# Attention steps spread by weight between expert-layer items, with three blocks of work put off

## Chip, cores and metric

One core of one Trainium2 chip runs the whole program. The metric is device time in microseconds (us) for one execution; the time before is the median of ten. A span is the time from the first to the last instruction of one execution, taken by the hardware profiler. The engines are PE (TensorE: matmuls and transposes; PEld is its weight load), DVE (VectorE), ACT (ScalarE), POOL (GpSimd) and SP (SyncE, which issues transfers). Each engine runs its own instructions in order and waits for others by semaphores.

## What is computed

Sliding-window attention with a linear bias for 8 batches, 8 heads, 576 positions of width 64, then a two-matrix layer with a swish between, over all 4608 rows:

```python
# q, k, v: (8, 8, 576, 64); window 128; slopes[h] = 2 ** -(h + 1)
scores = 1 / sqrt(64) * q @ k^T
scores = where(0 <= i - j < 128, scores - slopes[h] * |i - j|, -1e9)
attn = softmax(scores) @ v                     # per batch and head
x = attn.transpose(0, 2, 1, 3).reshape(4608, 512)
h = x @ w_in                                   # (4608, 2048)
out = (h * sigmoid(beta * h)) @ w_out          # (4608, 512), float32
```

## The kernel before

**Attention.** A batch has five row blocks (four of 128 rows and one of 64). Its work is cut into steps. `TP(b, p)` (L221) transposes a pair of heads of q and k on PE, eight transposes into two PSUM tiles, each copied out by DVE (L230); `TT` (L235) does the same for the last 64 rows. `SC(b, m, p)` (L258) computes scores of a pair of heads for half of the rows (`m`) into one PSUM tile of two banks (`psum_s`, one buffer), and ACT takes the exponential. For batches 0 and 1 (below `NPE`, which is 2) a table is added by matmuls (L263) and one exponential covers the tile (L285); from batch 2 on four exponentials with a bias do it (L290) and DVE multiplies by a mask (L294). `PV(b, qb, g)` (L306) multiplies by the values of four heads (L317, L321); DVE takes the reciprocal (L326) and scales (L327). `X(b, qb)` (L333) puts a finished row block, transposed, into `XT`, a ring of 1536 columns: for batches below `NTE`, which is 3, by four PE transposes (L345) and a copy (L350, on ACT for batch 0 and on DVE for 1 and 2), and from batch 3 on by a DMA transpose that SP issues (L341).

**The layer.** Rows go in nine groups of 512. `HS(g, j)` (L355) is an H item: four matmuls of 512 columns (L362), a tanh on ACT (L367), a combine on DVE (L368). `OS(g, i, n)` (L372) is an O item: four matmuls (L378), and after every fourth item an eviction by ACT (L384) and a store (L389), queued on POOL two items later. A group has 16 H and 16 O items. H of group g needs all of the group's 512 columns in `XT`.

**Loads.** SP issues q, k and the first two batches' v as float32 (L95, L109); POOL casts them (L113, L119, L129, L141). For batch 2 and later POOL issues v itself with the cast in the transfer (`load_v`, L136). From batch 3 on q and k are transposed by DMA transposes on SP (`TD`, L246). POOL also issues the first matrix in four chunks (`load_w1`, L189) and the second in four (`load_w2`, L192), and stores results.

**Order.** PE's order is the program's order throughout. The prologue runs batch 0's attention. Then `spread(hs(0), by_pair(1), 3, 0)` (L550) places batch 1's steps evenly by their number between the 16 H items of group 0. From L557 on SP's and POOL's orders are the program's too. There batch 2's values are issued (L558, before that the planner is free to put POOL's instructions elsewhere, and these five have a place among batch 1's casts), then all 16 H items of group 1 run with nothing between (L560), then batch 2's steps between the 16 O items of group 0 and the first 8 of group 1, then batch 3's steps among group 2's H items and the rest of group 1's O items, and so on, H of one group with O of the one before. `merge` (L435) adds each batch's loads, casts and DMA transposes as further entries of the list at fixed distances ahead of its first score step; a DMA `X` comes 2.5 steps after its place. `spread` (L408) counts all entries alike.

Of the kernel before, what the change touches and what calls it, by code (L numbers as in the profile page):

```python
# [11 lines left out]
BF16 = mybir.dt.bfloat16  # L12
F32 = mybir.dt.float32
P = 128
# [3 lines left out]
def kernel(  # L18
# [10 lines left out]
    nc = tc.nc  # L29
    B, H, S, D = q.shape  # L30
# [8 lines left out]
    NTE = 3  # L39
    LA = 4  # L40
    LM = P * LA
    NQB = 5
# [3 lines left out]
    TOKG = 512  # L46
    NTG = T // TOKG
# [8 lines left out]
    NPE = 2  # L56
# [3 lines left out]
    ident = const.tile([P, P], BF16, name="ident")  # L60
# [29 lines left out]
    staged = {}  # L90
# [98 lines left out]
        nc.gpsimd.dma_start(out=W1[:, :, bass.ts(n, 512)], in_=W1v[:, :, bass.ts(n, 512)])  # L189

    def load_w2(n):
        nc.gpsimd.dma_start(out=W2[:, bass.ts(n, 4), :], in_=W2v[:, bass.ts(n, 4), :])  # L192

    def late_consts():
        for m in range(2):
# [22 lines left out]

    pts, xns = {}, {}

    def TP(b, p):  # L221
        src = staged.pop((b, p))
        for i in range(2):
            tps = psum_t.tile([P, LA, P], BF16, name="tps", tag="t")
            for a in range(LA):
                nc.tensor.transpose(
                    out=tps[:, a, :], in_=src[:, i, a, :, :].rearrange("r h d -> r (h d)"),
                    identity=ident[:],
                )
            nc.vector.tensor_copy(  # L230
                out=QK[b % 2][:, i, p, 0:LM].rearrange("c (r a) -> c r a", a=LA),
                in_=tps[:].rearrange("c a r -> c r a"),
            )

    def TT(b):  # L235
        tps = psum_t.tile([P, 2, NP, P], BF16, name="tps", tag="t")
# [96 lines left out]
    def X(b, qb):  # L333
        nq = ROWS[qb]
        xnv = xns.pop((b, qb))[:].rearrange("p h d -> p (h d)")
        tok0 = (b * S + P * qb) % XTR
        n1 = min(nq, XTR - tok0)
        parts = [(tok0, 0, n1)] + ([(0, n1, nq)] if n1 < nq else [])
        if b >= NTE:
            for at, r0, r1 in parts:  # L340
                nc.sync.dma_start_transpose(out=XT[:, :, at : at + r1 - r0], in_=xnv[r0:r1, :])  # L341
            return
        xt = psum_t.tile([P, NDM, P], BF16, name="xt", tag="t")
        for c in range(NDM):
            nc.tensor.transpose(  # L345
                out=xt[:, c, :], in_=xnv[:, c * P : (c + 1) * P], identity=ident[:]
            )
        copy = nc.vector.tensor_copy if b else nc.scalar.copy
        for at, r0, r1 in parts:
            copy(out=XT[:, :, at : at + r1 - r0], in_=xt[:, :, r0:r1])  # L350


    gts, opss = {}, {}
# [47 lines left out]
    def flush():  # L401
        for e in list(stores):
            e[0] -= 1
            if e[0] < 0:
                e[1]()
                stores.remove(e)

    def spread(moe, todo, lead=0, tail=3):  # L408
        done, n = 0, len(moe)
        for i, it in enumerate(moe):  # L410
            flush()
            it()
            to = len(todo) * (i + 1 - lead) // (n - lead - tail)
            while done < min(len(todo), to):
                todo[done]()
                done += 1

    def sc(b, m, p):
        return lambda: SC(b, m, p)

    def pv(b, qb, g):
        return lambda: PV(b, qb, g)

    def x(b, qb):
        f = lambda: X(b, qb)
        at[b, qb] = f
        if b >= NTE:
            lazy.append(f)
        return f

# [25 lines left out]

    def by_pair(b):
        return [
            lambda: TP(b, 0), lambda: TP(b, 1), sc(b, 0, 0), lambda: TT(b), sc(b, 0, 1),
            lambda: TP(b, 2), sc(b, 1, 0), lambda: TP(b, 3), sc(b, 1, 1), pv(b, 0, 0), sc(b, 0, 2),  # L460
            pv(b, 1, 0), sc(b, 1, 2), pv(b, 2, 0), sc(b, 0, 3), pv(b, 3, 0), sc(b, 1, 3),
            pv(b, 4, 0), pv(b, 0, 1), pv(b, 1, 1), x(b, 0), pv(b, 2, 1), x(b, 1), pv(b, 3, 1),
            x(b, 2), pv(b, 4, 1), x(b, 3), x(b, 4),
        ]

    def by_block(b):

        e = b - 1
        r = [pv(e, 2, 1), pv(e, 3, 1), x(e, 2), sc(b, 0, 0), x(e, 3), pv(e, 4, 1), sc(b, 0, 1),
             x(e, 4)] if e >= NTE else [sc(b, 0, 0), sc(b, 0, 1)]  # L470
        return r + [
            sc(b, 0, 2), pv(b, 0, 0), sc(b, 0, 3), pv(b, 1, 0),
            pv(b, 0, 1), sc(b, 1, 0), x(b, 0), pv(b, 1, 1), sc(b, 1, 1), x(b, 1),
            sc(b, 1, 2), pv(b, 2, 0), sc(b, 1, 3), pv(b, 3, 0), pv(b, 4, 0),
        ]

    with tc.manual_schedule(engines={mybir.EngineType.PE}):

        for sb in range(NQB):
            c = load_v(0, sb)  # L480
            if sb == 3:
                with tc.issue_after(c.ins):
                    load_w1(0)
                    load_w1(1)
        for p in range(NP):
            c = load_pair(1, p, None if p else W1[0:1, 0, 0:1])
            if p % 2:
                with tc.issue_after(c.ins):
                    load_w1(2 + p // 2)
            if p == 1:  # L490
                load_tail(1)
        for sb in range(NQB):
            c = load_v(1, sb)
            if sb == 3:
                with tc.issue_after(c.ins):
                    for n in range(4):
                        load_w2(n)
        with tc.tile_pool(name="psum_x", bufs=2, space=bass.MemoryType.PSUM) as psum_x:
            pools = [psum_x, psum_x, psum_s]

            def sc0(m, p):
                SC(0, m, p, pools[0])
                pools.append(pools.pop(0))

            w = psum_t.tile([P, 512], F32, name="w", tag="t")
            idle(w[:], 9)
            TP(0, 0)
            TP(0, 1)
            sc0(0, 0)
            load_beta()  # L510
            TT(0)
            sc0(0, 1)
            TP(0, 2)
            sc0(1, 0)
            TP(0, 3)
            sc0(1, 1)
            for m in range(2):
                sc0(m, 2)
            for m in range(2):
                sc0(m, 3)  # L520
                PV(0, m, 0)
            for qb in (2, 3, 4):
                PV(0, qb, 0)
        psum_h = ctx.enter_context(
            tc.tile_pool(name="psum_h", bufs=2, space=bass.MemoryType.PSUM))
        psum_o = ctx.enter_context(
            tc.tile_pool(name="psum_o", bufs=2, space=bass.MemoryType.PSUM))
        w = psum_s.tile([P, 2, 512], F32, name="w", tag="sps")
        for qb in range(NQB):
            c = PV(0, qb, 1, (psum_o, "ops") if qb % 2 else (psum_h, "hps"))  # L530
            idle(w[:, 0, :], 1)
            if qb:
                X(0, qb - 1)
                idle(w[:, 1, :], 1)
        X(0, NQB - 1)
        with tc.issue_after(c.ins):
            late_consts()
        for p in range(NP):
            load_pair(2, p)
            if p == 1:  # L540
                load_tail(2)

        def hs(g):
            return [lambda j=j: HS(g, j) for j in range(NFF)]

        def os(g):
            return [lambda n=n: OS(g, n // 4, n % 4) for n in range(NFF)]


        spread(hs(0), by_pair(1), 3, 0)  # L550
        steps, first = by_pair(2), {}
        for b in range(NTE, B):
            first[b] = len(steps)
            steps += by_block(b)
        steps += [pv(B - 1, 2, 1), pv(B - 1, 3, 1), x(B - 1, 2), pv(B - 1, 4, 1), x(B - 1, 3),
                  x(B - 1, 4)]
        with tc.manual_schedule(engines={mybir.EngineType.SP, mybir.EngineType.Pool}):  # L557
            for sb in range(NQB):  # L558
                load_v(2, sb)
            for it in hs(1):  # L560
                it()
            todo, o1, done = merge(steps, first), os(1), 0
            for g in range(1, NTG):
                if g == 1:
                    moe = os(0) + o1[0:8]
                    end = todo.index(at[2, NQB - 1]) + 1
                elif g == 2:
                    moe = hs(2)
                    moe = sum((moe[2 * n : 2 * n + 2] + [o1[8 + n]] for n in range(8)), [])
                else:  # L570
                    moe = sum(([a, c] for a, c in zip(hs(g), os(g - 1))), [])
                if g > 1:
                    end = len(todo)
                    if g + 1 < NTG:
                        b, r = divmod(TOKG * (g + 2) - 1, S)
                        end = todo.index(at[b, r // P]) + 1
                spread(moe, todo[done:end], 0, 3 if g == 1 else 6)
                done = end
            while stores:
                flush()  # L580
            for it in os(NTG - 1):
                it()
# [30 lines left out]
```

## Time and profile before

| | us |
|---|---|
| median of ten runs | 351.59 |
| lowest, highest | 348.35, 355.66 |
| the profiled execution | 351.01 |
| its span, first to last instruction | 349.2 |
| H items of group 0 with batch 1 | 25.28 to 61.48 |
| H items of group 1 alone | 61.48 to 75.29 |
| O of group 0 and half of group 1, with batch 2 | 75.29 to 107.94 |
| H of group 2 and the rest of O of group 1, with batch 3 | 107.94 to 140.68 |
| the last attention step on PE | 293.5 |

The page gives each engine's busy time and the span in 40 slices of 8.7 us. A stage's limit is read from that stage: the idle time of an engine, and what ended it. PE's busy digits say little of its pace, since matmuls overlap; pace is read from the starts of items: an H item alone takes 13.81 / 16 = 0.86 us.

### The profile page before, as it was taken

Reading aid. Unit: us, or ns where it says so; the run is one execution under the profiler, and the core shown is the slowest. Engines: PE = TensorE matmul, PEld = TensorE weight load, DVE = VectorE, ACT = ScalarE, POOL = GpSimd, SP = SyncE. Lnnn points to the kernel's source line nnn. Section 1 sums busy time; section 2 is a strip of 40 time slices with the busy share of each in tenths; the row PEclk is TensorE's granted clock in tenths of the full one; section 3 lists DMA queues with packets and bytes.
Section 4 is the critical chain, followed back from the end, with each engine's and each line's share of the span. In section 5 each row is a group of like instructions: output and inputs, shape, how many; then the busy total and the mean of one; then the engine's idle time right before and its main releaser. Section 6 shows DMA issues by size and latency. Waiting matters only on the chain.

```text
span 349.2 us, 6129 instructions
## 1 busy us (share of the span) xinstructions
PE 324.5 (93%) x2237; PEld 154.1 (44%) x2279; DVE 197.3 (57%) x421; ACT 211.3 (61%) x407; POOL 107.6 (31%) x173
## 2 busy tenths in 40 slices
PE   6988967989997989999999999999999999999995
PEld 2454424444453344444444444444444444444442
DVE  6476728686653676565566656765666464444400
ACT  4655843657725695678568756876588654544411
POOL 7638545113364431323316332432000000100000
PEclk9899989999999899999999999999999999999999
DMA  7999999961999998999639994994123002010021
GB/s 198 238 172 248 172 236 220 221 146 46 171 187 215 205 167 163 168 164 158 138 82 202 173 211 111 171 180 93 40 68 61 31 32 68 30 62 30 30 88 65
DMA packets 138494, 47.67 MB, mean 137 GB/s; under 512 B 125648, under 2 KB 135904, under 8 KB 138464
## 3 DMA queue, kind: packets, MB, share of 16 engines
q1 hardware_dynamic: 103520, 31.15, 49.0%
q0 software_dynamic: 34912, 16.13, 35.0%
q8 instruction: 18, 0.29, 0.4%
q14 instruction: 12, 0.10, 0.1%
q10 hardware_dynamic: 32, 0.01, 0.0%
HBM read 36.71 MB, written 9.44 MB: 132 GB/s over the span
## 4 chain that ended last, share of the span: by engine, by line
PE 53%; DMA 19%; issue 10%; POOL 7%; SPq 4%; DVE 3%; ACT 3%; POOLq 0%
PE ops L378 24%; PE hps L362 23%; DMA fst<-in_q_dram 8%; DMA fst<-in_v_dram 5%; DMA fst<-in_k_dram 3%; POOL bst L129 3%; PE sps L277 3%; SPq L249 2%; ACT pt L290 2%; POOL vs L136 2%; DMA W<-in_moe_w_in_dram 2%; PE pv L321 1%; SPq L109 1%; PE pv L317 1%; DVE gT L368 1%
## 5 line engine op out<-in xcount | busy, mean ns | idle before, releaser
L367 ACT ACTIVATE sig<-hps,beta_h 128x512 bf16<-128x512 f32 x144 | 99.5, 692 | 80.5 <-PE hps L362 75.7
L362 PE MATMUL hps<-XT,W 128*128 128x512 bf16 x559 | 144.4, 383 | 1.3 <-DVE gT L368 0.3
L378 PE MATMUL ops<-W,gT 128*128 128x512 bf16 x555 | 142.4, 380 | 1.3 <-issue 0.3
L368 DVE SCALAR_TENSOR_TENSOR gT<-sig,hps 128x512 bf16<-128x512 bf16 x144 | 98.4, 684 | 69.1 <-ACT sig L367 68.8
L290 ACT ACTIVATE pt<-sps,bias 128x256 bf16<-128x256 f32 (+1 forms) x192 | 75.2, 479 | 11.9 <-PE sps L277 11.8
L362 PEld LDWEIGHTS <-W 128*128 128x128 bf16 x576 | 52.5, 98 | 59.1 <-issue 4.8
L378 PEld LDWEIGHTS <-gT 128*128 128x128 bf16 x576 | 52.2, 98 | 57.8 <-issue 2.4
L389 POOL DMA_DIRECT2D out_dram<-osb x32 | 17.9, 559 | 170.4 <-ACT osb L384 170.3
L294 DVE TENSOR_TENSOR pt<-pt,mask 128x1024 bf16<-128x1024 bf16 x48 | 35.8, 745 | 24.2 <-ACT pt L290 24.2
L129 POOL CAST bst<-fst 128x512 bf16<-128x512 f32 (+1 forms) x50 | 31.9, 659 | 26.6 <-DMA fst<-in_q_dram 20.2
L384 ACT ACTIVATE osb<-ops 128x512 f32<-128x512 f32 x36 | 21.7, 603 | 26.3 <-PE ops L378 26.3
L327 DVE TENSOR_TENSOR xn<-pv,zs 128x256 bf16<-128x256 f32 (+1 forms) x80 | 33.5, 420 | 2.1
L321 PE MATMUL pv<-vs,pt 128*128 128x65 bf16 x320 | 29.3, 195 | 4.2 <-POOL vs L141 2.1
L326 DVE RECIPROCAL zs<-pv 128x4 f32<-128x4 f32 (+1 forms) x80 | 14.0, 176 | 28.7 <-PE pv L321 28.0
L277 PE MATMUL sps<-qkT 64*128 64x256 bf16 (+2 forms) x320 | 26.0, 258 | 4.4 <-ACT pt L290 3.8
L321 PEld LDWEIGHTS <-pt 128*128 128x128 bf16 x320 | 21.9, 98 | 11.9 <-DVE pt L294 2.5
L317 PE MATMUL pv<-vs,pt 128*128 128x65 bf16 x256 | 24.5, 194 | 1.4 <-DVE xn L327 1.0
L136 POOL DMA_DIRECT2D vs<-in_v_dram x30 | 25.5, 854 | 0.5 <-issue 0.4
L277 PEld LDWEIGHTS <-qkT 64*128 64x128 bf16 x320 | 11.3, 95 | 31.5 <-issue 30.1
L317 PEld LDWEIGHTS <-pt 128*128 128x128 bf16 x256 | 19.8, 98 | 11.2 <-issue 3.1
L285 ACT ACTIVATE pt<-sps 128x1024 bf16<-128x1024 f32 x16 | 16.0, 1027 | 11.5 <-PE sps L277 11.1
L113 POOL CAST bst<-fst 128x512 bf16<-128x512 f32 x24 | 14.6, 623 | 11.7 <-DMA fst<-in_q_dram 6.5
(45 smaller groups left out, 103.7 us busy)
## 6 DMA issues: line engine op xcount, KB each, us to landing
fst<-in_q_dram SPq DMA_DIRECT2D x32, 256.0 KB, 4.5
fst<-in_k_dram SPq DMA_DIRECT2D x32, 256.0 KB, 5.1
out_dram<-osb POOLq DMA_DIRECT2D x32, 256.0 KB, 3.0
vs<-in_v_dram POOLq DMA_DIRECT2D x24, 128.0 KB, 5.9
fst<-in_v_dram SPq DMA_DIRECT2D x8, 256.0 KB, 7.7
W<-in_moe_w_in_dram POOLq DMA_DIRECT2D x4, 512.0 KB, 7.9
W<-in_moe_w_out_dram POOLq DMA_DIRECT2D x4, 512.0 KB, 15.2
fst<-in_q_dram SPq DMA_DIRECT2D x8, 128.0 KB, 5.2
```

What stands on the lines that cost most here:

```text
L129: nc.gpsimd.tensor_copy(out=t[0 : ROWS[sb], i], in_=f)
L136: nc.gpsimd.dma_start(out=VS[b % 2][0 : ROWS[sb], sb, :, 0:D], in_=v[b, :, P * sb : P * sb + ROWS[sb], :].rearrange("h p d -> p h d"),)
L277: nc.tensor.matmul(o, lhsT=qk[64 * e : 64 * e + 64, 1, p, P * kb : P * kb + P], rhs=qk[64 * e : 64 * e + 64, 0, p, P * kb : P * kb + nq], ...
L290: nc.scalar.activation(out=pt[:, e, cols], in_=sps[:, e, cols], func=ACTF.Exp, scale=qscale, bias=bias[:, half, h : h + 1],)
L294: nc.vector.tensor_tensor(out=pt[:], in0=pt[:], in1=masks[m][:].rearrange("p (o c) -> p o c", o=1).broadcast_to([P, 2, 512]), op=ALU.mult,)
L317: nc.tensor.matmul(pv[:, hl, 0 : D + 1], lhsT=weights(b, qb - 1, h, 1), rhs=vs[:, qb - 1, h, 0 : D + 1], start=True, stop=False,)
L321: nc.tensor.matmul(pv[:, hl, 0 : D + 1], lhsT=weights(b, qb, h, 0), rhs=vs[:, qb, h, 0 : D + 1], start=qb == 0, stop=True,)
L327: nc.vector.tensor_tensor(out=xn[0:nq, 4 * g : 4 * g + 4, :], in0=pv[0:nq, :, 0:D], in1=zs[0:nq].broadcast_to([nq, 4, D]), op=ALU.mult,)
L362: nc.tensor.matmul(hps[:], lhsT=W1[:, c, bass.ts(j, P)], rhs=XT[:, c, c0 : c0 + TOKG], start=(c == 0), stop=(c == NDM - 1),)
L367: nc.scalar.activation(out=sig[:], in_=hps[:], func=ACTF.Tanh, scale=beta_h[:, j : j + 1])
L368: nc.vector.scalar_tensor_tensor(out=gts[g][:, j, :], in0=sig[:], scalar=1.0, in1=hps[:], op0=ALU.add, op1=ALU.mult)
L378: nc.tensor.matmul(ops_[:], lhsT=gT[:, j, i * P : i * P + P], rhs=W2[:, j, :], start=(j == 0), stop=(j == NFF - 1),)
```

## The change

Transposing a pair is cut in two steps, one for q and one for k. Every step has a weight: 2 for a score step, 1 for a transpose step, a PV step or an X done on PE, 0 for loads and DMA transposes. `spread` places steps so that the weight done keeps pace with the items done, leaves `lead` items at the start and `tail` at the end without steps, and puts anything left after the last item. Batch 1's last row block (two PV and one X) is put off to group 1's H items. Group 1's H items are no longer alone: they form one list with group 0's O items and the first 8 of group 1, and batch 2's steps run among all 40. Batch 2's steps up to X of row block 2 are due there; the PV steps and X of its last row block and one PV and X of the fourth go in front of batch 3's. X goes by DMA transpose from batch 2 on, and the PE form copies on ACT. Batch 2's values are issued behind the second matrix. The last `tail` grows from 6 to 7 for later groups.

```diff
     def load_w2(n):
-        nc.gpsimd.dma_start(out=W2[:, bass.ts(n, 4), :], in_=W2v[:, bass.ts(n, 4), :])
+        return nc.gpsimd.dma_start(out=W2[:, bass.ts(n, 4), :], in_=W2v[:, bass.ts(n, 4), :])
...
-    def TP(b, p):
-        src = staged.pop((b, p))
-        for i in range(2):
-            tps = psum_t.tile([P, LA, P], BF16, name="tps", tag="t")
...
+    def TP(b, p, i):
+        src = staged[b, p]
+        tps = psum_t.tile([P, LA, P], BF16, name="tps", tag="t")
...
-        if b >= NTE:
+        if b >= NPE:
             for at, r0, r1 in parts:
                 nc.sync.dma_start_transpose(out=XT[:, :, at : at + r1 - r0], in_=xnv[r0:r1, :])
             return
...
-        copy = nc.vector.tensor_copy if b else nc.scalar.copy
         for at, r0, r1 in parts:
-            copy(out=XT[:, :, at : at + r1 - r0], in_=xt[:, :, r0:r1])
+            nc.scalar.copy(out=XT[:, :, at : at + r1 - r0], in_=xt[:, :, r0:r1])
...
+    cost = {}
+
     def spread(moe, todo, lead=0, tail=3):
-        done, n = 0, len(moe)
+        total, n = sum(cost.get(f, 0) for f in todo), len(moe) - lead - tail
+        done, k = 0, 0
         for i, it in enumerate(moe):
             flush()
             it()
-            to = len(todo) * (i + 1 - lead) // (n - lead - tail)
-            while done < min(len(todo), to):
-                todo[done]()
-                done += 1
+            while k < len(todo) and (i + 1 - lead >= n or (
+                done + cost.get(todo[k], 0)) * n <= total * (i + 1 - lead)):
+                done += cost.get(todo[k], 0)
+                todo[k]()
+                k += 1
+        for f in todo[k:]:
+            f()
+
+    def step(f, c):
+        cost[f] = c
+        return f
+
+    def tp(b, p, i):
+        return step(lambda: TP(b, p, i), 1)
+
+    def tt(b):
+        return step(lambda: TT(b), 1)
 
     def sc(b, m, p):
-        return lambda: SC(b, m, p)
+        return step(lambda: SC(b, m, p), 2)
 
     def pv(b, qb, g):
-        return lambda: PV(b, qb, g)
+        return step(lambda: PV(b, qb, g), 1)
 
     def x(b, qb):
-        f = lambda: X(b, qb)
+        f = step(lambda: X(b, qb), int(b < NPE))
         at[b, qb] = f
-        if b >= NTE:
+        if b >= NPE:
             lazy.append(f)
         return f
...
     def by_pair(b):
         return [
-            lambda: TP(b, 0), lambda: TP(b, 1), sc(b, 0, 0), lambda: TT(b), sc(b, 0, 1),
-            lambda: TP(b, 2), sc(b, 1, 0), lambda: TP(b, 3), sc(b, 1, 1), pv(b, 0, 0), sc(b, 0, 2),
-            pv(b, 1, 0), sc(b, 1, 2), pv(b, 2, 0), sc(b, 0, 3), pv(b, 3, 0), sc(b, 1, 3),
-            pv(b, 4, 0), pv(b, 0, 1), pv(b, 1, 1), x(b, 0), pv(b, 2, 1), x(b, 1), pv(b, 3, 1),
-            x(b, 2), pv(b, 4, 1), x(b, 3), x(b, 4),
+            tp(b, 0, 0), tp(b, 0, 1), sc(b, 0, 0), tp(b, 1, 0), tp(b, 1, 1), tt(b), sc(b, 0, 1),
+            tp(b, 2, 0), sc(b, 1, 0), tp(b, 2, 1), sc(b, 1, 1), tp(b, 3, 0), pv(b, 0, 0),
+            tp(b, 3, 1), sc(b, 0, 2), pv(b, 1, 0), sc(b, 1, 2), pv(b, 2, 0), sc(b, 0, 3),
+            pv(b, 3, 0), sc(b, 1, 3), pv(b, 0, 1), pv(b, 1, 1), x(b, 0), pv(b, 2, 1), x(b, 1),
+            pv(b, 3, 1), x(b, 2), x(b, 3), pv(b, 4, 0), pv(b, 4, 1), x(b, 4),
         ]
 
     def by_block(b):
 
         e = b - 1
-        r = [pv(e, 2, 1), pv(e, 3, 1), x(e, 2), sc(b, 0, 0), x(e, 3), pv(e, 4, 1), sc(b, 0, 1),
-             x(e, 4)] if e >= NTE else [sc(b, 0, 0), sc(b, 0, 1)]
+        if e < NTE:
+            r = [sc(b, 0, 0), pv(e, 3, 1), x(e, 3), pv(e, 4, 0), sc(b, 0, 1), pv(e, 4, 1), x(e, 4)]
+        else:
+            r = [pv(e, 2, 1), pv(e, 3, 1), x(e, 2), sc(b, 0, 0), x(e, 3), pv(e, 4, 1),
+                 sc(b, 0, 1), x(e, 4)]
...
-        spread(hs(0), by_pair(1), 3, 0)
-        steps, first = by_pair(2), {}
+        s1, s2 = by_pair(1), by_pair(2)
+        spread(hs(0), s1[:-3], 3, 2)
+
+        steps, first = s1[-3:] + [f for f in s2[:-3] if f not in (s2[-6], s2[-4])], {}
...
-            for sb in range(NQB):
+            with tc.issue_after(w2.ins):
+                load_v(2, 0)
+            for sb in range(1, NQB):
                 load_v(2, sb)
-            for it in hs(1):
-                it()
...
                 if g == 1:
-                    moe = os(0) + o1[0:8]
-                    end = todo.index(at[2, NQB - 1]) + 1
+                    moe = hs(1) + os(0) + o1[0:8]
...
-                if g > 1:
-                    end = len(todo)
-                    if g + 1 < NTG:
-                        b, r = divmod(TOKG * (g + 2) - 1, S)
-                        end = todo.index(at[b, r // P]) + 1
-                spread(moe, todo[done:end], 0, 3 if g == 1 else 6)
+                end = len(todo)
+                if g + 1 < NTG:
+                    b, r = divmod(TOKG * (g + 2) - 1, S)
+                    end = todo.index(at[b, r // P]) + 1
+                spread(moe, todo[done:end], 6 if g == 1 else 0, 7)
                 done = end
```

More of the change, by code (lines that the diff above doesn't have):

```diff
@@ L219 @@
     pts, xns = {}, {}
-    def TP(b, p):
-        src = staged.pop((b, p))
-        for i in range(2):
-            tps = psum_t.tile([P, LA, P], BF16, name="tps", tag="t")
[L225 to L232, printed above, removed]
-            )
+    def TP(b, p, i):
+        src = staged[b, p]
+        tps = psum_t.tile([P, LA, P], BF16, name="tps", tag="t")
+        for a in range(LA):
+            nc.tensor.transpose(
+                out=tps[:, a, :], in_=src[:, i, a, :, :].rearrange("r h d -> r (h d)"),
+                identity=ident[:],
+            )
+        nc.vector.tensor_copy(
+            out=QK[b % 2][:, i, p, 0:LM].rearrange("c (r a) -> c r a", a=LA),
+            in_=tps[:].rearrange("c a r -> c r a"),
+        )
     def TT(b):
@@ L496 @@
                     for n in range(4):
-                        load_w2(n)
+                        w2 = load_w2(n)
         with tc.tile_pool(name="psum_x", bufs=2, space=bass.MemoryType.PSUM) as psum_x:
@@ L506 @@
             idle(w[:], 9)
-            TP(0, 0)
-            TP(0, 1)
+            TP(0, 0, 0)
+            TP(0, 0, 1)
+            TP(0, 1, 0)
+            TP(0, 1, 1)
             sc0(0, 0)
@@ L512 @@
             sc0(0, 1)
-            TP(0, 2)
+            TP(0, 2, 0)
+            TP(0, 2, 1)
             sc0(1, 0)
-            TP(0, 3)
+            TP(0, 3, 0)
+            TP(0, 3, 1)
             sc0(1, 1)
```

## The prediction

> **What bounds the kernel now.** I read the page's busy shares first, then the busy times by stage, then the longest waits of TensorE (PE) stage by stage, then the order of PE and GpSimd (POOL) around each of those waits.
>
> The page's first two parts (engine, busy us, share, instructions; then tenths of 40 slices):
>
> ```profile
> PE 324.5 (93%) x2237; PEld 154.1 (44%) x2279; DVE 197.3 (57%) x421; ACT 211.3 (61%) x407; POOL 107.6 (31%) x173
> PE   6988967989997989999999999999999999999995
> PEclk9899989999999899999999999999999999999999
> ```
>
> PE is the bound, but its holes lie in the first 16 slices (up to 140 us); after that it is full and its clock is whole. The same by stage. I cut at the first hidden product H(0) (25.28), the first of H(1) (61.48), the first output product O(0) (75.29), the first of H(2) (107.94) and the first of H(3) (140.68):
>
> ```profile
> 25.28:61.48 36.20, 29.28 (x249) 14.92 (x253) 22.91 (x62) 19.50 (x25) 21.40 (x33) 0.95 1.32 223
> 61.48:75.29 13.81, 13.76 (x66) 6.26 (x64) 9.91 (x15) 10.29 (x15) 2.46 (x4) 1.00 0.98 188
> 75.29:107.94 32.65, 30.20 (x264) 16.12 (x268) 19.98 (x44) 15.92 (x39) 13.47 (x21) 1.00 1.21 150
> 107.94:140.68 32.74, 28.70 (x202) 12.87 (x205) 20.72 (x42) 24.91 (x54) 11.70 (x16) 0.95 1.20 178
> ```
>
> Columns: stretch, length, busy PE, PEld, DVE, ACT, POOL, granted PE clock, DMA share, GB/s. I call the stages A, B, C, D, and what follows E. A loses 6.9 us of PE time to idling and 5% of its clock; B loses nothing; C loses 2.4; D loses 4.0 and again 5%. In A DMA runs over its full share (1.32). In D ACT is busy 24.91 of 32.74 us, so it is nearly the second bound there. Two waits with what follows them, on PE:
>
> ```profile
> 46.76 0.19 PE L317 MATMUL pv<-vs,pt 128*128 128x65 bf16 x1
> 49.07 0.19 PE L321 MATMUL pv<-vs,pt 128*128 128x65 bf16 x1 [2.12 <-POOL vs L141]
> 50.56 1.89 PE L362 MATMUL hps<-XT,W 128*128 128x512 bf16 x4
> ...
> 111.21 0.39 PE L277 MATMUL sps<-qkT 64*128 64x256 bf16 x4
> 113.26 0.39 PE L277 MATMUL sps<-qkT 64*128 64x256 bf16 x4 [1.66 <-ACT pt L290]
> 114.76 1.90 PE L362 MATMUL hps<-XT,W 128*128 128x512 bf16 x4
> ```
>
> The first waits for a row block of batch 1's values; the second is a score step put straight behind another, with one PSUM buffer that four exponentials must empty. After each, four matmuls take 1.9 us where they take 1.03 elsewhere. The clock in those places:
>
> ```profile
> 50.00:51.00 1.00, 0.98 (x8) 0.45 (x9) 0.72 (x2) 0.33 (x1) 1.00 (x2) 0.50 1.10 351
> 115.00:116.00 1.00, 1.00 (x3) 0.30 (x2) 0.97 (x3) 0.84 (x2) 0.41 (x1) 0.50 2.05 179
> ```
>
> So a wait of about 2 us is paid twice: 5% of 36.2 is 1.8 us in A, 5% of 32.74 is 1.6 in D. Why the values were late, on POOL:
>
> ```profile
> 38.67 0.70 POOL L136 DMA_DIRECT2D vs<-in_v_dram  x1
> 43.17 0.61 POOL L141 CAST vs<-fst 128x512 bf16<-128x512 f32 x1 [1.88 <-DMA fst<-in_v_dram]
> 48.41 0.62 POOL L141 CAST vs<-fst 128x512 bf16<-128x512 f32 x1 [4.62 <-DMA fst<-in_v_dram]
> ```
>
> Batch 1's values arrive 2.5 us apart and the fourth 5.2, while batch 2's (L136, issued at 27.08, 31.34, 32.77, 34.75, 38.67) share the DMA engines.
>
> **The change part by part.** Prices of steps on PE, from start to start in its timeline: an H or O item 0.864 (13.81 / 16), four transposes 0.23, a score step 0.33 (batch 1, with table matmuls: 0.85), a PV step 0.24.
>
> Batch 2's values behind W2. This takes five POOL issues of 0.84 (4.2 us) and their transfers out of 27 to 50 us and puts them between the last casts of batch 2's q and k. On POOL's DMA queue W1's third chunk landed at 38.67, three V loads at 41.13, 43.30, 45.15, W1's last chunk at 48.89; without them the last needs 48.89 - 45.15 = 3.7 us after 38.67, about 42.4. Batch 1's fourth value block at the former 2.5 us spacing is there at 45.6, perhaps before. PE, faster by the other parts, wants the last W1 chunk at about 46 and that block at about 44. So of 2.12 + 0.36 idle and 1.8 of clock I give back 1.0 idle and 0.9 clock. What is late next: W2 (landed 59.26 to 70.41) and, behind it, batch 2's values.
>
> Transposes of q and k split in halves, each behind other work. In A it removes the waits of 0.79 (POOL's cast) and 0.81 (DVE's copy) at 30 and 31 us: 1.6. In C it removes 0.79 + 0.22. A second H item now always lies between score steps of batch 1, which removes 0.77 at 45.0. The copies themselves (0.68 each on DVE) stay; in A DVE is busy 22.91 of 36.20, which covers them. If A shrinks to 30 us, that is three quarters.
>
> Batch 1's X copies go from DVE (four of 0.41 and one of 0.29) to ACT (0.59 and 0.37): ACT gains 2.7 us in A and B, where it has 19.50 of 36.20 and 10.29 of 13.81; on the path only the copy just before H(1): two H items (1.73) cover it, and I take 0. X(1,3) still follows closely on its PV, so the wait of 1.02 at 61.15 stays; 0.41 + 0.24 go.
>
> Batch 1's last blocks (two PV, one X with its four transposes) move from A to B: 2 x 0.24 + 0.23 = 0.7 less in A, 0.7 more in B.
>
> Batch 2's X as DMA transposes. Off PE: five times 0.23 = 1.15 in C. Off DVE: 1.9. Added to SP: five issues of 1.21 (6.1 us), landing 3.3 us after issue at the median, 6.7 at most. X(2,1) and X(2,2) stand behind the two transposes of batch 3's last rows, which wait for a POOL cast, which stands behind the third store, which waits for ACT. The third store can go about 12 items (10.5 us) before H(2); then value issue and cast 2.0, two transposes 2.4, two X 2.4, landing 2 to 4: done 0 to 2 us ahead of H(2). I take 0, bounds 0 and +3.
>
> H(1) joined with O(0) and half of O(1): 40 items hold what 24 held, less two PV (0.5) moved to D, plus the first score step of batch 3 (0.33). C waited 1.2 us in four places for ACT between score steps with one O item between (a score step's four exponentials are 4 x 0.478 = 1.9); now two O items or one with transposes lie between most. Of C's 2.2 us of waits I take 1.4 as gone. B + C: -1.15 - 1.4 + 0.7 + 0.33 - 0.5 = -2.0; bounds -3 and +1.
>
> D. The two adjacent score steps are gone: -1.66 and the clock, -1.6. One score step less, two PV more: +0.2. But the new order still has seven score steps with one to three items between, and ACT needs 1.9 + 0.69 for each H item, 2.6 to 3.3 us, against PE's 1.5 to 3.2: the remaining 2.1 us of waits stay, and I add 0.6. D: -2.5; bounds -5.2 (all waits and the clock) and +2 (waits of about 1 us at most score steps).
>
> E. Waits there are only 2.1 us. By the instruction order five pairs of score steps have just one H and one O item between, three before: two times about 0.3 us. E: +0.5; bounds -1.5 and +2.
>
> A: -1.6 - 0.77 - 1.5 (values) - 0.9 (clock) - 0.65 - 0.7 = -6.1; bounds -8 (all but the 1.02) and -1.5 (loads hold PE).
>
> Sum: -6.1 - 2.0 - 2.5 + 0.5 = -10.1. The profiled execution took 351.01 (span 349.2, 1.8 around it): 340.9. It lies 0.6 under the median 351.59, so I predict **341.5**.
>
> Two pages of the Trainium skill speak otherwise. "TensorE: Matmul & The Clock Gate", section "HAM oscillation — how this bites in real kernels", says that idle gaps up to some 3.4 us leave the clock alone. The rows above show 0.50 after gaps of 2.12 and 1.66; by the page none of the 2.5 us of clock would come back, and the sum would be 344. "VectorE: DVE Perf Modes", section "Rules for kernel authors", says to transpose 128x128 on TensorE if PSUM will do, and by DMA otherwise, which is against moving batch 2's X. Here four cost PE 0.23 us and a DMA transpose lands 3.3 after its issue; by the page the 1.15 would not be worth the wait, and the sum would be about 342.7.
>
> **Rivals.** *Loads hold stage A.* PE gets ahead of W1 and batch 1's values; A gives only -1.5: 346. For it: the DMA share of 1.32 in A and 12.2 us from issue to landing of W1's last chunk. Against it: the three V loads that leave are just those ahead of that chunk.
>
> *Batch 2's values too late.* If W2's last chunk lands at 70.4 as before and five V loads follow at 2.1 us each, the last lands at 81; the first PV of batch 2 comes about 22 us after H(1) begins, near 77. About 3 us of waiting and 1.5 of clock: 346. Against it: batch 1's values, and so W2's issue behind them, come earlier.
>
> *X of batch 2 holds H(2): slower.* If the cast of batch 3's last rows is caught behind stores (POOL has stood 12.09 us at one, until 84.17), X(2,2) follows a store three further on, each about 3.5 to 4 us: 12 us later, plus clock 1.6. 341.5 + 13.5 = 355. It decides once X(2,2) lands more than 10 us after H(2) could begin; up to there it only eats the gain.
>
> *Weights change the order and not the waits:* B to D give nothing, and A what its loads allow (-1.5): about 350.
>
> **How the numbers follow.** Forecast 0.58, its own range 335.5 to 344.5 (the bounds of A and D do not fall together). Loads 0.17, values 0.10, nothing gained 0.07, X late 0.08. Range **335.5 to 348.5**, which reaches over the two middle rivals. A measurement can tell 0.5% (349.8 and 353.3) from no change: faster 0.84, same 0.08, slower 0.08.
>
> **What would show it.** A some 30 us long, no wait on values at its two thirds, PE clock whole there; W1's last chunk landed before 46 us; no DVE copy into XT; in D no wait over 1.2 us for exponentials and a whole clock; H(2) starting without a wait for a DMA. I am wrong if PE waits on W, vs or XT at those places, if D stays above 32 us, or if E grows by over 2 us.

## The result and the profile after

The changed kernel takes 348.55 us (median of 15 runs, 343.83 to 350.27), the kernel before 351.84 (median of 52, 347.82 to 355.66). The ratio is 0.9875, with an interval of 0.9842 to 0.9908: faster by 1.25%, where 341.5 us would have been 2.9%. Medians here are of all executions and ratios of those in the faster of two states alone, so a ratio is not the quotient of two medians. The median lies 0.05 us above the range: on which side of that edge it fell is chance, with single executions from 343.83 to 350.27, but the 7 us to the forecast are not. The profiled execution took 348.75 us, with a span of 346.3 and a mean granted clock of 0.979.

The page of the changed kernel first: the span, the engines' busy shares, PE's busy tenths and granted clock by slices of 8.7 us, and the group of H matmuls with the idle time ahead of it.

```profile
span 346.3 us, 6108 instructions
...
PE 323.0 (93%) x2216; PEld 152.9 (44%) x2259; DVE 194.0 (56%) x411; ACT 213.6 (62%) x412; POOL 106.6 (31%) x173
...
PE   5989998999998894999999999999999999999995
PEclk9699999999999997899999999999999999999999
...
L360 PE MATMUL hps<-XT,W 128*128 128x512 bf16 x556 | 144.4, 383 | 5.5 <-DMA XT<-xn 4.6
```

The holes of the first ten slices are mostly gone. A new one has come: the 16th slice (130 to 139 us) is only four tenths busy, it and the next have a lowered clock, and the group's line names a wait of 4.6 us for a DMA into XT, which the kernel before did not have.

The stages, cut at the same instructions as before: H(0) at 26.67, H(1) at 55.46, O(0) at 73.24, H(2) at 99.67, H(3) at 134.50 us. E is in two lines, so that its clock can be seen. Columns: stretch, length, busy time of PE, PEld, DVE, ACT and POOL, granted clock, DMA share, GB/s.

```profile
26.67:55.46 28.79, 26.29 (x229) 13.63 (x233) 19.71 (x52) 20.79 (x28) 17.09 (x28) 1.00 1.19 239
55.46:73.24 17.78, 17.07 (x120) 8.60 (x121) 15.58 (x27) 13.32 (x25) 7.16 (x10) 1.00 1.51 174
73.24:99.67 26.43, 25.98 (x199) 12.44 (x201) 12.76 (x30) 15.00 (x37) 12.67 (x19) 1.00 1.47 198
99.67:134.50 34.83, 27.19 (x213) 12.73 (x216) 22.14 (x46) 24.08 (x51) 15.19 (x22) 0.99 1.20 182
134.50:142.07 7.57, 7.57 (x29) 2.93 (x30) 1.97 (x4) 1.37 (x2) 0.00 (x0) 0.61 1.42 157
142.07:346.30 204.23, 197.07 (x1232) 91.21 (x1256) 106.19 (x205) 125.03 (x246) 39.41 (x63) 1.00 0.60 98
```

Set against the stages of before and the forecast of each (us):

| stage | before | after | change | forecast |
|---|---|---|---|---|
| up to H(0) | 25.28 | 26.67 | +1.39 | 0 |
| A | 36.20 | 28.79 | -7.4 | -6.1 |
| B + C | 46.46 | 44.21 | -2.25 | -2.0 |
| D | 32.74 | 34.83 | +2.1 | -2.5 |
| E | 208.5 | 211.8 | +3.3 | +0.5 |
| around the span | 1.8 | 2.45 | +0.65 | 0 |

The table's changes sum to -2.3, which is 351.01 to 348.75. A, B and C did what was forecast, and a little more. Up to H(0) the kernels do the same work; that point lay between 26.0 and 27.9 us in the other profiles of this study, so the +1.39 is not put down to the change. The difference is in D and E. PE's timeline there (start, duration, line, and in brackets the idle time before and what ended it):

```profile
128.89 1.03 PE L376 MATMUL ops<-W,gT 128*128 128x512 bf16 x4
134.50 1.86 PE L360 MATMUL hps<-XT,W 128*128 128x512 bf16 x4 [4.58 <-DMA XT<-xn]
136.16 1.91 PE L376 MATMUL ops<-W,gT 128*128 128x512 bf16 x4
```

D ends with 4.58 us of waiting, and four matmuls then take 1.86 us, not 1.03. Without the wait D is 30.25 us, 2.5 less than before: the forecast. With a clock of 0.61 over 7.57 us, E pays 0.39 x 7.57 = 2.95 us; the remaining +0.35 stands against a forecast of +0.5. The miss in this pair of profiles is thus one wait and what follows it, 4.58 + 2.95 = 7.5 us.

What the wait hung on is shown by the chain of waits of the changed kernel, between 121 and 135 us (start, duration, what):

```profile
122.09 0.97 SPq L340
...
123.11 3.76 DMA fst<-in_q_dram
...
126.99 0.61 POOL bst L129
...
127.81 0.62 POOL bst L129
128.44 1.64 SPq L248
...
130.18 1.22 SPq L248
...
131.50 2.87 DMA XT<-xn
...
134.50 1.86 PE hps L360 x4
```

Read backwards: H(3) needs X(3,2), the third row block of batch 3 put into XT (a join, for short), a DMA transpose on SP. SP issued it at 131.50, straight behind the two transposes (L248) of a later batch's row block. Those waited for POOL's casts, and these for a load that SP had issued at 123.11, behind other transposes and an X. So SP's stream, in which loads, TD and X stand in one fixed order, had come to this step too late. In the kernel before, the same step stood at the same place of that stream:

```profile
133.24 2.83 SPq L249 DMA_TRANSPOSE qkT<-bst  x2
136.17 3.41 SPq L341 DMA_TRANSPOSE XT<-xn  x2
```

There it landed at 139.37, and H(3) began at 140.68: a margin of 1.3 us, while PE was forecast to reach H(3) some 10 us sooner.

### The profile page after: what moved, and what is told of

It reads as the page before. It is cut to its first block, busy times and chain, and to the rows that moved or that the text cites. A ratio compares the mean times of both kernels' runs of the same rounds, so it can differ in the third digit from the quotient of the medians.

```text
span 346.3 us, 6108 instructions
## 1 busy us (share of the span) xinstructions
PE 323.0 (93%) x2216; PEld 152.9 (44%) x2259; DVE 194.0 (56%) x411; ACT 213.6 (62%) x412; POOL 106.6 (31%) x173
## 4 chain that ended last, share of the span: by engine, by line
PE 82%; DVE 5%; DMA 4%; ACT 4%; issue 2%; SPq 2%; another core or an unknown queue 1%; POOL 1%; POOLq 0%
PE hps L360 33%; PE ops L376 33%; PE sps L276 6%; PE pv L320 3%; PE sps L262 2%; PE pv L316 2%; ACT pt L289 2%; DVE xn L326 2%; PE tps L225 2%; DMA fst<-in_k_dram 2%; DVE pt L293 2%; ACT sig L365 1%; DMA fst<-in_q_dram 1%; DVE gT L366 1%
## 5 line engine op out<-in xcount | busy, mean ns | idle before, releaser
L293 DVE TENSOR_TENSOR pt<-pt,mask 128x1024 bf16<-128x1024 bf16 x48 | 34.3, 714 | 14.6 <-ACT pt L289 14.3
L129 POOL CAST bst<-fst 128x512 bf16<-128x512 f32 (+1 forms) x50 | 30.9, 637 | 35.5 <-DMA fst<-in_q_dram 18.9
L229 DVE COPY qkT<-tps 128x512 bf16<-128x512 bf16 x24 | 16.2, 687 | 6.6 <-PE tps L225 6.4
```

Of the source, the lines that this page charges most:

```text
L129: nc.gpsimd.tensor_copy(out=t[0 : ROWS[sb], i], in_=f)
L293: nc.vector.tensor_tensor(out=pt[:], in0=pt[:], in1=masks[m][:].rearrange("p (o c) -> p o c", o=1).broadcast_to([P, 2, 512]), op=ALU.mult,)
```

## The experiments

All runs are compared with runs of the kernel before on the same chip, whose medians were 353.0, 352.8 and 352.3 us in the three sets.

| run | what | us | ratio to before (interval) |
|---|---|---|---|
| changed kernel | | 348.55 | 0.9875 (0.9842 to 0.9908) |
| e1_x_before_td | X(3,2) ahead of the two transposes | 347.37 | 0.9889 (0.9807 to 0.9971) |
| e2_x2_on_pe | batch 2's X back on PE | 343.78 | 0.9794 (0.9730 to 0.9858) |
| e3_v2_early | batch 2's values as before | 350.25 | 0.9966 (0.9920 to 1.0012) |
| e4_warm | PE kept busy during the wait | 348.78 | 0.9911 (0.9844 to 0.9977) |
| x2_twice | batch 2's X issued twice | 356.14 | 1.0135 (1.0074 to 1.0196) |
| x2_three_dma | three of batch 2's X by DMA | 343.78 | 0.9777 (0.9734 to 0.9821) |
| tail_11 | steps of H(2) end sooner | 346.36 | 0.9827 (0.9794 to 0.9860) |
| before_v2_late | before, values behind W2 | 348.33 | 0.9888 (0.9862 to 0.9915) |
| e2_equal_weights | e2, every entry weighs 1, loads too | 344.99 | 0.9825 (0.9773 to 0.9876) |
| e2_pairs_unsplit | e2, q and k transposed together | 345.25 | 0.9834 (0.9786 to 0.9882) |
| e2_v2_early | e2, batch 2's values as before | 348.14 | 0.9867 (0.9825 to 0.9910) |
| e2_x_sooner | e2, lag of the DMA joins 1.5 | 344.14 | 0.9765 (0.9733 to 0.9796) |

**Is it the place of X(3,2) on SP's queue, or the amount of work there?** The theory was that the five added issues hold back the whole stream; the rival, that X(3,2) has merely an unlucky place. (The expectation counts the rival as theory 1.)

```
 # e1_x_before_td, in merge
-                jobs.append((i + 2.5, f))
+                jobs.append((i + 2.4, f))
```

> The changed kernel with one number altered: a DMA transpose X comes 2.4 instead of 2.5 steps after its place, which only turns ties, so that X(3,2) stands on SP ahead of the two transposes of batch 5's first rows (TD(5,0)) and not behind them. Theory 1 (X(3,2) was late because of its place on SP): it issues some 3 us earlier (128.4 instead of 131.5), PE's wait of 4.58 us at the first H item of group 3 falls to 1 to 2 us and most of the halved clock after it (0.61 over 7.6 us, 3 us) goes: span 340 to 343. Theory 2 (X(3,2) is late because its input or SP's whole stream is late): the wait stays above 3 us, span 345 to 347.

Two lines of PE's timeline in this run:

```profile
131.01 1.02 PE L360 MATMUL hps<-XT,W 128*128 128x512 bf16 x4 [1.17 <-DMA XT<-xn]
...
200.99 1.03 PE L360 MATMUL hps<-XT,W 128*128 128x512 bf16 x4 [3.23 <-DMA XT<-xn]
```

X(3,2) was issued at 127.02, and the wait before H(3) fell to 1.17 us. But H(5) now waits 3.23 for its X, with half the clock behind it, and a third wait of 1.16 follows at 237. The span is 346.3 us, as in the changed kernel and not the 340 to 343 of theory 1, and the ratio can't be told from the changed kernel's. The place decides which group waits; the delay of the stream remains.

```
 # e2_x2_on_pe, in X and in x
-        if b >= NPE:
+        if b >= NTE:
...
-        f = step(lambda: X(b, qb), int(b < NPE))
+        f = step(lambda: X(b, qb), int(b < NTE))
```

> The changed kernel with batch 2's X back on PE (20 transposes, copies on ACT), so SP has five transposes fewer, 6 us of issuing. Theory A (those five held up SP's stream, and X(3,2) with it): SP comes to X(3,2) 3 to 6 us earlier, the wait before H(3) falls under 1.5 us, the clock stays whole there, PE pays 1.15 us for the transposes: span 340 to 342. Theory B (SP waits for loads and casts anyway, so its length does not matter): X(3,2) is issued within 1.5 us of 131.5, the wait stays above 3 us, and the span is 347 to 348.

SP's timeline in this run, then stage D and the stretch around H(3) (columns as above):

```profile
125.25 2.86 SPq L248 DMA_TRANSPOSE qkT<-bst  x2
128.21 3.33 SPq L340 DMA_TRANSPOSE XT<-xn  x2
```

```profile
99.02:132.09 33.07, 28.65 (x233) 13.61 (x237) 22.26 (x48) 25.55 (x56) 11.82 (x17) 1.00 1.12 166
132.00:140.00 8.00, 7.76 (x48) 3.43 (x47) 4.22 (x8) 5.23 (x12) 3.47 (x5) 1.00 1.19 176
```

With the five joins on PE and ACT, X(3,2) is issued 3.3 us sooner, H(3) begins at 132.09 without a wait, and the clock stays whole. The span falls by 4.8 us to 341.5 and not by the 7.5 of the wait and the clock, since the joins cost PE something too: B to D takes 43.90 + 33.07 = 76.97 us here, and 44.21 + 30.25 = 74.46 in the changed kernel without its wait. The ratio falls from 0.9875 to 0.9794, and the intervals just overlap (0.9842 to 0.9858). The next two runs vary the amount.

```
 # x2_twice, in X, after the DMA transpose
+    scr = const.tile([P, NDM, P], BF16, name="scr")
...
+                if b == 2:
+                    nc.sync.dma_start_transpose(out=scr[:, :, 0 : r1 - r0], in_=xnv[r0:r1, :])
 # x2_three_dma, in place of b >= NPE in X and in x
+    def by_dma(b, qb):
+        return b >= NTE or b == 2 and qb < 3
```

> The changed kernel with each DMA transpose X of batch 2 issued a second time, into a scratch tile that nothing reads: SP gets five more transposes (6 us of issuing, and a wait of up to 3 us where two follow each other). If SP's own stream sets when X(3,2) is issued, it comes 5 to 9 us later than 131.5, PE's wait before H(3) grows from 4.6 to 9 to 13 us, and the span is 350 to 356. If loads and casts set it, X(3,2) comes within 2 us of 131.5 and the span stays within 2 us of 346.3.

> The changed kernel with batch 2's last two X back on PE and the first three still DMA transposes: SP has three more than with none, two fewer than the changed kernel (2.4 us). If each costs SP its issue, X(3,2) comes 2 to 3 us earlier than 131.5 and PE's wait before H(3) is 1 to 2.5 us, between 4.6 (all five) and 0 (none): span 342 to 345. If it takes none of them or all to matter, the wait is 0 or still above 4.

PE's timeline of the doubled kernel (the extra copies go to a tile that nobody reads), and X(3,2) on its SP:

```profile
101.59 1.04 PE L363 MATMUL hps<-XT,W 128*128 128x512 bf16 x3 [2.14 <-DMA XT<-xn]
...
141.26 1.01 PE L363 MATMUL hps<-XT,W 128*128 128x512 bf16 x2 [8.03 <-DMA XT<-xn]
```

```profile
138.54 2.52 SPq L341 DMA_TRANSPOSE XT<-xn  x2
```

And of the kernel with three:

```profile
132.13 1.02 PE L363 MATMUL hps<-XT,W 128*128 128x512 bf16 x4 [0.44 <-DMA XT<-xn]
```

Zero, three, five and ten DMA transposes of batch 2 give a wait before H(3) of none, 0.44, 4.58 and 8.03 us, and with ten also 2.14 before H(2), the place that the prediction had looked at. Doubling makes the kernel slower than before, 1.35% over it. The doubled run changes SP's queue alone, and X(3,2) is issued 7.0 us later, for 6 us of added issuing (part may come by way of PE, which the wait before H(2) holds up). That such issues push X(3,2) back, and that H(3) then waits for it, is shown.

The waits are not the dose itself, for PE does not come to H(3) at the same time in the four kernels. Counted from each one's H(0), with none, three, five and ten:

| us after H(0) | none | three | five | ten |
|---|---|---|---|---|
| X(3,2) landed | 105.1 | 104.3 | 107.7 | 114.7 |
| PE was ready for H(3) | 105.8 | 104.0 | 103.2 | 107.0 |

Three cost X(3,2) nothing that can be seen (so the wait was 0.44 and not the expected 1 to 2.5), five 2.6 us and ten 9.7. The other half of the 4.58 us is that PE, freed of the joins, is ready 2.5 us sooner than with none. With ten it is late itself, after its wait before H(2), which is why the wait is under the expected 9 to 13.

**Does the half clock cost what the profile shows?** PE was given 21 matmuls on zeros ahead of H(3), into a buffer that nobody reads.

```
 # e4_warm, in the loop over groups
+                if g == 3:
+                    w = psum_t.tile([P, 512], F32, name="w", tag="t")
+                    idle(w[:], 21)
```

> The changed kernel with 21 matmuls on zeros, 512 columns each (4.5 us), before the first H item of group 3; they add nothing to the result. PE then has no idle time there, and the wait itself stays. If the halved clock from 134 to 141 us comes from that wait's idling, the clock stays 1.00 there and the span falls by about 3 us, to 343 to 344. If the clock falls for another reason, the span stays 346 to 348 and the clock in the stretch is again near 0.6.

PE's timeline and the stretch behind it:

```profile
129.72 4.70 PE L214 MATMUL w<-zero 128*128 128x512 bf16 x21
```

```profile
134.50:142.00 7.50, 7.37 (x46) 3.22 (x46) 3.37 (x7) 4.36 (x9) 0.00 (x0) 1.00 1.36 194
```

In the profile H(3) begins at 134.25 (134.50 in the changed kernel), the clock stays whole, and the span falls by 3.2 us to 343.1, as expected. The 12 timed runs do not show it (344.89 to 353.67, median 348.78). Five of the 12 have a mean clock of 0.981 to 0.985 all the same. The runs of the changed kernel themselves speak for the price: of the sixteen executions on record, nine with a mean clock of 0.978 to 0.983 have a median span of 347.1, seven with 0.990 to 0.995 of 344.2. That is a correlation and not an intervention, and what the zero matmuls cost in the other executions wasn't seen. So the 2.95 us is what one profile shows; over all runs it stays open.

**Would ending H(2)'s steps sooner do?**

```
 # tail_11
-                spread(moe, todo[done:end], 6 if g == 1 else 0, 7)
+                spread(moe, todo[done:end], 6 if g == 1 else 0, 11 if g == 2 else 7)
```

> The changed kernel with group 2's steps done four items (3.5 us) earlier, 11 items without steps at the end instead of 7; SP's order is the same. If X(3,2) is late because it waits for its own PV steps, it comes some 3 us earlier and the wait falls to 1 to 2 us (span 342 to 344, less 0 to 2 us of new waits for exponentials in stage D). If SP's stream ahead of it sets the moment, X(3,2) stays at 131 to 132 and the span at 345.5 to 348.

PE's waits between 95 and 142 us in this run (engine, line and releaser; total, times, longest):

```profile
PE sps L276 <- ACT pt L289: 2.1, 3, 0.7
PE hps L360 <- DMA XT<-xn: 1.2, 1, 1.2
```

X(3,2) did not come sooner (131.93). Denser score steps made PE wait for ACT instead (2.1 us, where the changed kernel has 0.9 in D), so it arrived later, waited 1.24 us and kept its clock. X(3,2) thus kept the moment that the second theory gives, while the profile's span of 343.3 is the first theory's; PE's own lateness hides the wait, which was not foreseen.

**What are the other parts worth?** Batch 2's values were put back to their old place in the changed kernel and in e2, and moved alone in the kernel before.

```
 # e3_v2_early and e2_v2_early
-            with tc.issue_after(w2.ins):
-                load_v(2, 0)
-            for sb in range(1, NQB):
+            for sb in range(NQB):
                 load_v(2, sb)
 # before_v2_late: the same lines the other way, in the kernel before
```

> The changed kernel with batch 2's five value transfers back among batch 1's casts. My account of stage A says that their moving took away the wait for batch 1's fourth value block, 2.5 us, and the clock of 1.8: stage A (26.7 to 55.5) would be 3 to 5 us longer again. If the end is set by X(3,2) on SP, less of it shows in the whole: span 346 to 349. If instead stage A was shortened by the split transposes and the weights alone, stage A stays within 1 us of 28.8 and the span within 1 us of 346.3.

> The version with batch 2's X on PE, with batch 2's values back among batch 1's casts. There is no wait for X before H(3) to hide it, so what the move is worth shows in the whole: the wait of 2.7 us for batch 1's values comes back, with or without a halved clock after it (1.8): span 344 to 346.5, median ratio 0.5 to 1.3% above that version's 0.979. If it stays under 342.5 the move is worth nothing.

> The kernel before with one part alone of the change: batch 2's values behind W2. Stage A loses the wait for batch 1's values (2.5 us) and the halved clock after it (1.8): span 349.2 - 3 to 4.5 = 344.5 to 346.5, if all else follows. In the kernel before X(3,2) landed 1.3 us before the first H item of group 3; if SP's stream sets that moment and does not move up with PE, a wait of 1 to 3 us for XT appears there and the span is 346.5 to 348.5.

PE's timeline of e3, and stage A of before with only the values moved:

```profile
49.62 0.19 PE L320 MATMUL pv<-vs,pt 128*128 128x65 bf16 x1 [2.66 <-POOL vs L141]
```

```profile
26.03:58.31 32.28, 27.80 (x248) 14.41 (x252) 22.91 (x63) 19.43 (x25) 19.79 (x32) 1.00 1.19 248
```

With the old place the wait for batch 1's values is back, 2.66 us and longer than the 2.12 before, because PE, counted from H(0), comes 0.9 us sooner and the values only 0.3. Stage A is 31.73 us long, 2.9 more than in the changed kernel; this time the clock stayed whole behind the wait. Moved alone, the values shorten A from 36.2 to 32.3 us and give the kernel a ratio of 0.9888, nearly the whole measured gain of the full change. What lies behind stage A takes 287.7 us in the kernel before and 287.8 in this run. There H(3) waits too, 1.07 us for X(3,2), with no join of batch 2 on SP: PE was ready for it at 136.24 and not at 140.68, 4.4 us sooner, and X(3,2) landed only 2.2 us sooner, at 137.22. In e2 the move is worth 0.9867 - 0.9794 = 0.7%, with overlapping intervals.

```
 # e2_equal_weights, in spread
-        total, n = sum(cost.get(f, 0) for f in todo), len(moe) - lead - tail
+        total, n = len(todo), len(moe) - lead - tail
...
-                done += cost.get(todo[k], 0)
+                done += 1
 # e2_pairs_unsplit, in by_pair (tp2 does both halves in one step of weight 2)
+            tp2(b, 0), tp2(b, 1), sc(b, 0, 0), tt(b), sc(b, 0, 1), tp2(b, 2), sc(b, 1, 0),
...
 # e2_x_sooner, in merge
-                jobs.append((i + 2.5, f))
+                jobs.append((i + 1.5, f))
```

> The version with batch 2's X on PE, with every entry of the list counted alike (loads and DMA transposes too), as the kernel before did; the order of steps and all else stay. If the weights carry part of the gain: adjacent or nearly adjacent score steps come back, PE's waits for exponentials grow by 2 to 4 us in stages B to D, perhaps with a halved clock: span 343.5 to 347 against 341.5. If the weights do not matter, the span stays within 1 us of 341.5.

> The version with batch 2's X on PE, with the transposes of a pair of heads again one step (q and k together, weight 2) in the former order. My step took 1.6 us in stage A and 1.0 in C for the split. With it undone: waits of PE for DVE's copies and POOL's casts of 0.7 to 2.6 us come back, span 342 to 344. If the join with H(1) and the weights had already spread them, the span stays within 0.7 us of 341.5.

> The version with batch 2's X on PE, with each DMA transpose X one step sooner (1.5 instead of 2.5 after its place), so most stand ahead of the neighbouring transposes of q and k. That version has no wait for XT left, so I expect nothing: span 341 to 342. If X in front makes SP wait for its input and holds loads back, new waits come later: span 342.5 to 345.

Equal weights are 0.3% and unsplit pairs 0.4% above e2, both within the intervals: neither part has a price that these runs can tell from none, though the profile of the unsplit kernel has waits of 0.81, 0.88 and 0.67 us at 32.5, 42.2 and 68.8 back. A smaller lag changes nothing. The versions e2, x2_three_dma and e2_x_sooner (0.979, 0.978, 0.977) can't be told apart; they are the fastest here, about 2% under the kernel before, and the last two lie below the changed kernel with no overlap.

## Why the prediction was wrong

**The step that failed** is "Batch 2's X as DMA transposes", with its "I take 0, bounds 0 and +3". The five issues were priced by whether X(2,1) and X(2,2) would be in time for H(2). They were: X(2,2) landed at 98.89 and H(2) began at 99.67, inside the forecast "0 to 2 us ahead". But the issues also push back what stands behind them on SP: loads, the transposes of the next batches, and X(3,2) for H(3). The prediction asked this for H(2) alone. The margin could be read from the trace of before: X(3,2) landed at 139.37, H(3) at 140.68. A PE forecast to come 10.6 us sooner there (6.1 + 2.0 + 2.5) had 1.3 us of cover, unless SP's stream came sooner too. It did, but by less: X(3,2) landed 5.0 us sooner, at 134.36, and 8.0 sooner in e2, at 131.40. So the term taken as 0 was 4.58 us of waiting and, in the profile, 2.95 of clock, of which taking the joins back to PE returned 4.8. Part of it would probably have come without them, as the 1.07 us of before_v2_late show: the gain itself uses up the margin. e2 takes 343.78 us, near the upper end of the forecast's own range.

**What held.** Stage A: -7.4 for -6.1. W1's last chunk landed at 42.35 (forecast 42.4), the fourth block of batch 1's values was cast at 43.99 (forecast 45.6 or before), and PE did not wait for it. The clock there is whole. The move of the values was under-sized: alone the move shortens A by 3.9 us, where 1.5 + 0.9 was forecast for it, and the other edits take the remaining 3.5, where 3.7 was forecast. Taken out of the changed kernel (e3) it is worth 2.9; there the clock behind the wait stayed whole. B + C: -2.25 for -2.0. D without the one wait: -2.5 as forecast (in e2, which has no wait for XT, D takes 33.07 us, two of the joins on PE included), and PE's idle time there besides that wait is 34.83 - 27.19 - 4.58 = 3.06 us, where 4.0 - 1.66 + 0.6 = 2.9 was forecast. It has changed its kind: score steps wait 0.9 for ACT (2.6 before), PV steps 1.6 for their masks (0.6 before). E without the clock: +0.35 for +0.5.

**The rivals.** "Loads hold stage A" fell: no wait for W or values in A. "Batch 2's values too late" fell: the last landed at 75.03, and the first PV of batch 2 began at 78.87. "Weights change the order and not the waits" fell with A to C, though the runs of e2 show no separate price for weights or splitting. "X of batch 2 holds H(2)" had the right mechanism, a join caught behind other work on SP and the clock after it, but one group too early: in the changed kernel it costs 7.5 us in the profile and eats the gain, and only with ten issues did it make the kernel slower.

**The two pages.** The Trainium skill, "VectorE: DVE Perf Modes", section "Rules for kernel authors", prefers TensorE for a 128x128 transpose if PSUM will do. The prediction priced that rule at 1.2 us and set it aside; here it was right for the five together, e2 against the changed kernel, though for a reason that the rule does not give: the queue, not the transpose. With three of the five by DMA (x2_three_dma) the kernel is as fast as e2. "TensorE: Matmul & The Clock Gate", section "HAM oscillation — how this bites in real kernels", would have kept the clock whole after the short gaps; the half clock after 4.58 us agrees with it, and the gaps near 2 us, whose numbers stand in the last section, do not. After 2.66 us in e3 the clock stayed whole, as the page has it and against the prediction's reading that a wait of about 2 us is paid twice.

## What to carry to other kernels

Before work is moved to a queue that runs in a fixed order, list what stands behind it there for the next two uses and not only for the first: each one's landing against the time at which its user starts, with the user moved up by the forecast gain. A margin of 1.3 us is soon used up by a speed-up that the queue shares only in part: in before_v2_late, with nothing added to SP, PE came 4.4 us sooner and already waited 1.07. Where a doubled dose of the suspect and a smaller one are cheap to build, they settle more than moving one item in the queue, which here only moved the wait to a later group.

## What the hardware showed beyond that

The granted clock fell to half after gaps of 2.12 and 1.66 us in the kernel before, 2.14 and 8.03 in x2_twice, 3.23 in e1, 4.45 in e3 (before H(3)) and 4.58 in the changed kernel. But the same score step with the same gap of 1.66 us in before_v2_late did not lower it, nor did 2.66 us in e3 or 1.68 and 1.61 in e2_v2_early. The length of a gap alone does not decide it.

In all fourteen profiles the clock changes on a grid: the moments of change within one execution lie 3.41 us or a multiple of it apart, in the kernel before 49.53, 52.94, 114.38 and 117.80 (64.85 us is 19 times 3.413), and these half clocks are 3.41 us long, 6.83 (after 4.58) or 10.24 (around 8.03). Laid on that grid, two stretches of before with what followed, then the gap and the stretches of before_v2_late (PE's busy time is the second number, the granted clock the third from the end):

```profile
46.12:49.53 3.41, 1.29 (x13) 0.69 (x12) 0.05 (x1) 1.53 (x2) 1.12 (x2) 1.00 1.31 224
49.53:52.94 3.41, 2.94 (x19) 1.34 (x19) 1.15 (x3) 1.48 (x2) 3.41 (x6) 0.50 1.24 261
110.97:114.38 3.41, 1.67 (x13) 0.81 (x13) 1.98 (x3) 2.93 (x8) 0.68 (x1) 1.00 1.21 205
114.38:117.80 3.42, 3.42 (x16) 1.08 (x14) 2.19 (x5) 2.56 (x7) 1.97 (x3) 0.50 1.70 182
```

```profile
110.07 0.39 PE L277 MATMUL sps<-qkT 64*128 64x256 bf16 x4 [1.66 <-ACT pt L290]
110.40 1.04 PE L362 MATMUL hps<-XT,W 128*128 128x512 bf16 x4
```

```profile
108.16:111.58 3.42, 1.76 (x17) 0.83 (x14) 1.83 (x3) 2.94 (x8) 0.41 (x1) 1.00 1.27 224
111.58:115.00 3.42, 3.26 (x25) 1.45 (x24) 3.25 (x8) 3.24 (x9) 1.60 (x3) 1.00 1.75 152
```

The gap of 2.66 us in e3 falls across two stretches:

```profile
44.46:47.87 3.41, 2.25 (x20) 1.02 (x19) 1.20 (x3) 2.62 (x4) 0.32 (x1) 1.00 1.30 224
47.87:51.29 3.42, 1.68 (x22) 0.90 (x22) 1.23 (x4) 0.50 (x1) 2.34 (x4) 1.00 1.17 245
```

From H(0) to 325 us, the half clock followed every stretch in which PE was busy for 1.29 us or less (1.23 in x2_twice and 0.88 in e1 too). Of the four next ones, with 1.58 (e2_v2_early), 1.67, 1.68 and 1.76 us, only that with 1.67 was followed by it. A stretch at half clock was the last where PE was busy for 2.94 us or more of it, and another followed after 2.56 (changed kernel) and 2.20 (x2_twice). So in these profiles it seems to count how much of a gap falls into one stretch of 3.41 us, and a gap near 2 us costs the clock or not by where it lies. The busy times are modelled and no run here was made to test this, so what decides near 1.7 us stays open.
